# Two products a key chunk instead of three in the second batch's attention, with the sums of the exponentials taken by VectorE

## The chip, the core and the metric

The kernel runs on one core of one Trainium2 chip. The metric is the device time in microseconds (us) of one execution; the kernel before takes 920.13 us, the median of 3 runs (919.63 to 921.04).

## The reference, cut to what matters

Three layers follow each other: an attention whose queries are averaged in pairs, a mixture of four experts (w1, ReLU, w2, weighted by `domain_probs`), and a gated layer (`w_gate`, `w_val`, `w_out`). The change is in the first:

```
B, H, S, D = 2, 8, 1152, 64
q_pool = q.reshape(B, H, S // 2, 2, D).mean(axis=3)
scores = scale * np.matmul(q_pool, k.transpose(0, 1, 3, 2))
scores = scores - np.max(scores, axis=-1, keepdims=True)
attn = np.exp(scores)
attn = attn / (np.sum(attn, axis=-1, keepdims=True) + 1e-09)
return np.matmul(attn, v)
```

So every query needs a weighted sum of the values (the numerator) and the sum of its exponentials (the denominator).

## The kernel before

**Work and stages.** Products are made exact enough by splitting an fp32 operand into a high half (type F32R) and a low half, the rest. The attention is cut into 32 units `u`: 16 for each batch, each one head and 288 of its 576 pooled queries. A unit has its 1152 keys in nine chunks `c` of 128 partitions, so a score tile `s` holds 9 x 288 numbers a partition, in three groups `g` of three chunks. In order, a unit goes through `scores` (two products a chunk), `copy_scores` (ScalarE), `max_scores` (VectorE), `turn_max`, `reduce_max` and `spread_max` (the maximum over all keys, transposed and spread by TensorE), `subtract`, `expo`, and `av`, the product with the values. The experts of a batch (1536 products in all, `experts`, through the helper `gemm` at L864) need that batch's whole attention. The first batch's experts run beside the second batch's attention; then the second batch's experts run alone, and then the gated layer.

**The products with the values (L588).** In the first batch one plain fp32 product a chunk is made: the stationary tile holds 64 columns of values beside 64 columns of ones, so that the same product gives the numerator in 64 rows of the result and the denominator in the other 64. In the second batch, exponentials and values are split (`half_hi`, `half_lo` give `eh` and `el`; `prep_v` gives the halves of the values), and three F32R products a chunk are made: `vh`·`eh`, `vl`·`eh`, `vh`·`el`. `vh` has 64 columns of ones beside the high halves and `vl` 64 columns of zeros beside the low halves (`open_v`, L390, fills them by GpSimd). `take_part` (L608) then moves the numerator (ScalarE, tile `num`) and the denominator plus 1e-9 (VectorE, tile `den`) out of PSUM; after two units, `invert` makes the reciprocal of `den` (VectorE, two halves) and `scale` multiplies (GpSimd, into `xst`). `split_x` (L343) splits `xst` for the experts, for the second batch on ScalarE and VectorE.

**The order of the work.** Inside `tc.manual_schedule()` (L1097) the class `Plan` writes out one order for every engine. Each step is entered with a due time, an engine, a planned cost in us and its tiles (`at`, L60). `arrange` (L101) then simulates the engines: whenever one is free it takes, among the steps that are ready, the one due first. Steps that are ready are not held back for their due time (SP's loads are), so due times are priorities. The steps of unit `u` are due at `9 * u` plus one of the constants at L27 to L39; the `n`-th expert product of the first batch is due at `E0_START + n / E0_RATE` (L1103). A step's due time is never earlier than that of the steps whose tiles it reads or writes. Tiles with one buffer are handed on in the order of the due times (`takes`): PSUM bank `d` passes from `turn_max` to `spread_max` and to the transposes of the next keys and queries, bank `c` holds the running `av`, and there are three score tiles `s`. Steps marked `port` are kept from overlapping each other on VectorE and GpSimd in the simulation. The engines then run their lists in order. The second batch's experts and the gated layer come after the plan, in a fixed order.

Of the kernel before, what the change touches and what calls it, by code (L numbers as in the profile page):

```python
# [21 lines left out]
TOP = (1.875 - 2.0**-23) * 2.0**-96  # L22
# [1 line left out]

MT, TOP, MB, MCOPY = 10.23, 11.11, 11.18, 12.05  # L27
SUB = (11.07, 10.75, 13.58)
EXP = ((13.43, 16.94, 15.82), (12.68, 14.5, 17.57))
HALF_HI = (14.41, 16.21, 16.25)  # L30
HALF_LO = (13.1, 15.0, 17.1)
AV = (17.93, 15.5)
FINISH = (22.33, 24.2)
SHARE = (0.7, 2.54, 2.4, 3.2, 3.7)
COPY, MAX = 0.94, 0.25
PREP_Q, PREP_K = (4.3, 5.58, 0.4), (6.33, -0.27)
SPLIT = (-9.69, -6)
E0_START = 159.71
E0_RATE = 9.69  # L39
LAST = 18  # L40


class Plan:
# [8 lines left out]
    def __init__(self, room):  # L52
        self.room = room
        self.psum = ("sc", "av", "m")

        self.shared = ("v", "vh", "vl")
# [107 lines left out]
def tile_kernel(  # L164
# [13 lines left out]
    nc = tc.nc  # L178
    P = 128
    B, H, S, D = q.shape  # L180
# [4 lines left out]
    W = 288  # L185
# [3 lines left out]
    KC = S // P  # L189
    NPAIR = H // 2  # L190
# [29 lines left out]
    def single(tag, name):  # L220
        return psum.tile([P, 512], F32, tag=tag, name=name)
# [113 lines left out]
    at = plan.at  # L335
# [5 lines left out]
    vts, vlos = {}, {}  # L341

    def split_x(b, j, sl, hi=True, lo=True):  # L343
        if b not in xts:
# [13 lines left out]
    def where(u):  # L358

        jj, r = divmod(u, 2 * NH)  # L360
        half, i = divmod(r, 2)
        return jj // NPAIR, jj, half, i
# [27 lines left out]
    def open_v(which, i):  # L390

        tiles = vlos if which else vts
        tiles[f"h{i}"] = t = raw.tile(
            [P, KC, 2, D], F32R, tag=f"v{2 * which + i}", name=f"v{'hl'[which]}{i}"
        )
        nc.gpsimd.memset(t[:, :, 1 - i, :].bitcast(F32), 0.0 if which else 1.0)

    def prep_v(jj, i, lower):
        vr = vraws[jj, i]
        hi = vts[f"h{i}"][:, :, i, :]  # L400
        if not lower:
            nc.scalar.activation(out=hi, in_=vr, func=AF.Copy)
            return
        nc.gpsimd.tensor_tensor(
            out=vlos[f"h{i}"][:, :, i, :], in0=vr, in1=hi.bitcast(F32), op=ALU.subtract
        )


    spare = [acc.tile([QT, 2, NQT, 2 * D], F32, tag="acc", name="qraw1")]
# [178 lines left out]
    def av(u, chunks):  # L588
        b, jj, _, i = where(u)
        if u not in avs:  # L590
            avs[u] = single("c", "av")
        for c in chunks:
            if b:
                hi, lo = (h[:, c % 3, :] for h in parts[u, c // 3])
                vh, vl = vts[f"h{i}"], vlos[f"h{i}"]
                terms = [(vh, hi), (vl, hi), (vh, lo)]
            else:
                terms = [(vts[jj % 2 * 2 + i], stiles[u][:, c, :])]
            for n, (w, e) in enumerate(terms):
                nc.tensor.matmul(  # L600
                    avs[u][:, :W],
                    w[:, c].rearrange("p t d -> p (t d)"),
                    e,
                    start=(c == 0 and n == 0),
                    stop=(c == KC - 1 and n == len(terms) - 1),
                )

    def take_part(u, n):  # L608

        i = where(u)[3]  # L610
        name = ("num", "den")[n]
        if i == 0:
            pairs[u // 2, n] = small.tile([P, W], F32, tag=name, name=f"{name}{u}", bufs=1)
        me, other = slice(i * D, (i + 1) * D), slice((1 - i) * D, (2 - i) * D)
        t = pairs[u // 2, n][me]
        if n:
            nc.vector.tensor_scalar_add(t, avs[u][other, :W], EPS)
        else:
            nc.scalar.activation(out=t, in_=avs[u][me, :W], func=AF.Copy)

    def invert(u, n):
        den = pairs[u // 2, 1]
# [13 lines left out]
    def plan_attention():  # L636
# [61 lines left out]
        for u in range(B * UPB):  # L698
            t = KC * u
# [44 lines left out]
            for g in range(3):  # L744
                chunks = range(3 * g, 3 * g + 3)
                at(
                    t + SUB[g], "POOL" if g else "DVE", 2.05 if g else 1.05, subtract, u, g,
                    kind="port" if g else None,
                    reads=[("mc" if g else "m", u)], writes=[("s", u, c) for c in chunks],
                    uses=[("S", u)],  # L750
                )
                at(
                    t + EXP[b][g], "ACT", 0.925, expo, u, g,
                    writes=[("s", u, c) for c in chunks], uses=[("S", u)],
                )
# [14 lines left out]
                for cs in [chunks] if b == 0 else [[c] for c in chunks]:  # L770
                    at(
                        t + AV[b] + cs[0], "PE", 1.46 if b == 0 else 0.397, av, u, cs,
                        kind="r" if b else "f",
                        reads=[("eh", u, g), ("el", u, g), ("vh", i), ("vl", i)]
                        if b
                        else [("s", u, c) for c in cs] + [("v", jj % 2 * 2 + i)],
                        writes=[("av", u)],
                        takes=[("c", ("av", u))] if cs[0] == 0 else [],
                        uses=[("S", u)],
                    )  # L780
            end = t + FINISH[b]
            p = u // 2
            for n in range(2):
                tag = ("num", "den")[n]
                at(
                    end, ("ACT", "DVE")[n], (0.405, 0.455)[n], take_part, u, n,
                    reads=[("av", u)], writes=[(tag, p, i)], takes=[] if i else [(tag, (tag, p, 2))],
                    uses=[(tag, p, 2)],
                )
            if i == 1:  # L790
                for n in range(2):
# [45 lines left out]
        for jj in range(NPAIR, B * NPAIR):  # L837
            t = 4 * KC * jj
            for i in range(2):
                ready = t + 6.7 + KC * i  # L840
                at(
                    ready - 7, "SP", 0.5, load_vraw, jj, i,
                    writes=[("vr", jj, i)], takes=[("vraw", ("vr", jj, i))],
                )
                if jj == NPAIR:
                    for which, when in enumerate((20, 0.2)):
                        at(
                            ready - when, "POOL", 0.58, open_v, which, i,
                            takes=[(f"v{2 * which + i}", ("V", which, i))],
                            writes=[("v", 2 * which + i)],  # L850
                        )
                at(
                    ready, "ACT", 0.68, prep_v, jj, i, False,
                    reads=[("vr", jj, i), ("v", i)], writes=[("vh", i)],
                )
                at(
                    ready, "POOL", 1.45, prep_v, jj, i, True, kind="port",
                    reads=[("vr", jj, i), ("vh", i), ("v", 2 + i)], writes=[("vl", i)],
                )
# [321 lines left out]
```

## Time and profile before

| what | us |
|---|---|
| median of 3 runs | 920.13 |
| the profiled execution's own time | 921.15 |
| its span in the trace | 919.4 |
| TensorE busy in the span | 884.4 |
| VectorE busy | 576.6 |
| ScalarE busy | 462.0 |
| GpSimd busy | 388.4 |

The profile names the engines PE (TensorE; PEld is its weight load, which overlaps), DVE (VectorE), ACT (ScalarE), POOL (GpSimd) and SP (SyncE, which issues the loads). A group of instructions is printed as line, engine, operation, output and inputs, shapes, count, busy time and the mean duration of one in ns; behind the bar stands the engine's idle time just before them and what ended it. The duration that is printed for one matmul spans its passage through the array, and consecutive ones overlap; the time that a matmul takes from the engine is read from a run of them.

### The profile page before, as it was taken

The page shows a single profiled execution, that of the slowest core. Times are in us where ns is not written, and L with a number is a line of the kernel's source. Part 1 is how long each engine was busy: PE and PEld are TensorE (multiplying, and loading weights), DVE is VectorE, ACT ScalarE, POOL GpSimd, SP SyncE. Part 2 cuts the span into 40 slices and gives each one's busy share as a digit, 9 for nine tenths or more (in the row PEclk, how much of TensorE's full clock was granted, in tenths as well). Part 3 has the DMA queues.
Part 4 walks back from the last instruction along what each step waited for, and adds up shares of the span by engine and source line. Part 5 has one row for each costly group of instructions (what it writes and reads, how often), then busy time and mean ns, then how long its engine had stood idle before and what let it go on. Part 6 is the DMA issues. An engine that isn't in the chain of part 4 may idle for free.

```text
span 919.4 us, 14986 instructions
## 1 busy us (share of the span) xinstructions
PE 884.4 (96%) x5916; PEld 842.3 (92%) x5916; DVE 576.6 (63%) x883; ACT 462.0 (50%) x786; POOL 388.4 (42%) x266
## 2 busy tenths in 40 slices
PE   4899998999999999999999999999999999999998
PEld 3667777899999999999999999999999999999886
DVE  4678778776667577675664334333468988888800
ACT  4678778877776767666633222232323333333110
POOL 2465657867776796778631000203023333222000
PEclk9999999999999999999999999999999999999999
DMA  5012221323233223111243232323333323223210
GB/s 141 2 41 67 49 74 39 101 71 86 72 84 92 65 73 83 46 59 60 60 148 96 89 95 81 94 88 87 92 93 99 107 70 91 92 77 98 78 69 34
DMA packets 124149, 72.30 MB, mean 79 GB/s; under 512 B 32304, under 2 KB 119344, under 8 KB 124080
## 3 DMA queue, kind: packets, MB, share of 16 engines
q1 hardware_dynamic: 124080, 71.36, 26.7%
q8 instruction: 46, 0.75, 0.3%
q14 instruction: 23, 0.19, 0.1%
HBM read 68.96 MB, written 2.38 MB: 78 GB/s over the span
## 4 chain that ended last, share of the span: by engine, by line
PE 89%; DVE 5%; ACT 3%; issue 2%; DMA 1%; POOL 1%; SPq 0%; DVEq 0%; ACTq 0%; POOLq 0%
PE ps L864 43%; PE g L864 16%; PE av L600 12%; PE o L864 8%; PE sc L494 3%; PE sc L495 3%; DVE acc L522 1%; PE mt L528 1%; ACT s L511 1%; PE tr L438 1%; PE tr L464 1%; DVE kt L456 1%; PE m L550 1%; ACT s L573 1%; DVE s L567 1%
## 5 line engine op out<-in xcount | busy, mean ns | idle before, releaser
L306 ACT ACTIVATE whi<-wraw 128x512 fp32r<-128x512 f32 x128 | 80.4, 629 | 174.6 <-PE ps L864 157.1
L567 POOL TENSOR_TENSOR s<-s,m 128x864 f32<-128x864 f32 x64 | 132.2, 2085 | 76.3 <-ACT m L560 76.2
L864 PE MATMUL ps<-xhi,whi 128*128 128x288 f32 x512 | 153.0, 299 | 0.0
L864 PE MATMUL ps<-hhi,whi 128*128 128x288 f32 x512 | 152.2, 297 | 0.0
L864 PE MATMUL ps<-hhi,wlo 128*128 128x288 f32 x512 | 151.1, 295 | 0.0
L864 PE MATMUL ps<-xhi,wlo 128*128 128x288 f32 x512 | 151.0, 295 | 0.0
L864 PE MATMUL ps<-xlo,whi 128*128 128x288 f32 x512 | 150.9, 295 | 0.0
L864 PE MATMUL ps<-hlo,whi 128*128 128x288 f32 x512 | 150.9, 295 | 0.0
L313 DVE TENSOR_TENSOR wlo<-wraw,whi 128x512 fp32r<-128x512 f32 x96 | 81.9, 853 | 101.1 <-ACT whi L306 101.1
L931 POOL TENSOR_TENSOR yacc<-yacc,yt 128x576 f32<-128x576 f32 x24 | 41.3, 1722 | 187.8 <-DVE yt L925 187.8
L511 ACT ACTIVATE s<-sc 128x576 f32<-128x576 f32 (+1 forms) x160 | 93.5, 600 | 47.6 <-PE sc L495 45.9
L573 ACT ACTIVATE s<-s 128x864 f32<-128x864 f32 x96 | 87.7, 921 | 18.4 <-DVE s L567 13.8
L864 PE MATMUL g<-yhi,wlo 128*128 128x384 f32 x288 | 96.3, 334 | 0.5 <-DVE wlo L313 0.5
L864 PE MATMUL g<-yhi,whi 128*128 128x384 f32 x288 | 96.2, 334 | 0.5 <-ACT yhi L1022 0.5
L864 PE MATMUL g<-ylo,whi 128*128 128x384 f32 x288 | 96.2, 334 | 0.0
L864 PEld LDWEIGHTS ps<-xlo,whi 128*128 128x128 f32 x512 | 96.2, 188 | 0.0
L864 PEld LDWEIGHTS ps<-hlo,whi 128*128 128x128 f32 x512 | 96.1, 188 | 0.0
L864 PEld LDWEIGHTS ps<-hhi,whi 128*128 128x128 f32 x512 | 96.1, 188 | 0.0
L864 PEld LDWEIGHTS ps<-xhi,whi 128*128 128x128 f32 x512 | 96.1, 188 | 0.0
L864 PEld LDWEIGHTS ps<-xhi,wlo 128*128 128x128 f32 x512 | 96.1, 188 | 0.0
L864 PEld LDWEIGHTS ps<-hhi,wlo 128*128 128x128 f32 x512 | 96.1, 188 | 0.0
L494 PE MATMUL sc<-qhi,kt 128*128 128x288 f32 x288 | 88.2, 322 | 4.7 <-ACT s L511 1.9
(94 smaller groups left out, 1950.7 us busy)
## 6 DMA issues: line engine op xcount, KB each, us to landing
wraw<-in_moe_w_dram SPq DMA_DIRECT2D x128, 256.0 KB, 2.7
w<-in_moe_w_gate_dram SPq DMA_DIRECT2D x12, 512.0 KB, 3.9
w<-in_moe_w_val_dram SPq DMA_DIRECT2D x12, 512.0 KB, 3.6
w<-in_moe_w_out_dram SPq DMA_DIRECT2D x12, 512.0 KB, 3.5
qraw<-in_q_dram SPq DMA_DIRECT2D x32, 144.0 KB, 2.4
kraw<-in_k_dram SPq DMA_DIRECT2D x14, 288.0 KB, 3.9
v<-in_v_dram SPq DMA_DIRECT2D x8, 288.0 KB, 4.2
vraw<-in_v_dram SPq DMA_DIRECT2D x8, 288.0 KB, 3.0
```

What stands on the lines that cost most here:

```text
L306: nc.scalar.activation(out=hi, in_=t, func=AF.Copy)
L313: eng.tensor_tensor(out=lo, in0=t, in1=hi.bitcast(F32), op=ALU.subtract)
L438: nc.tensor.matmul(pt[:, m * P : (m + 1) * P], kr[:, c].rearrange("p h d -> p (h d)"), ident, is_transpose=True,)
L456: nc.vector.tensor_tensor(out=kt[other, sl], in0=pt[me, : 3 * P], in1=kt[me, sl].bitcast(F32), op=ALU.subtract)
L494: nc.tensor.matmul(ps, wt, qhi, start=True, stop=False)
L495: nc.tensor.matmul(ps, wt, qlo, start=False, stop=True)
L511: nc.scalar.activation(out=s[:, c : c + n, :], in_=ps[:, :n, :W], func=AF.Copy)
L567: eng.tensor_tensor(out=sg, in0=sg, in1=m.unsqueeze(1).to_broadcast([P, 3, W]), op=ALU.subtract)
L573: nc.scalar.activation(out=sg, in_=sg, func=AF.Exp)
L600: nc.tensor.matmul(avs[u][:, :W], w[:, c].rearrange("p t d -> p (t d)"), e, start=(c == 0 and n == 0), stop=(c == KC - 1 and n == len(term ...
L864: nc.tensor.matmul(ps, w, x, start=first and n == 0, stop=last and n == len(terms) - 1)
L931: nc.gpsimd.tensor_tensor(out=y, in0=y, in1=yts[o], op=ALU.add)
```

## The change

Second batch only: `vl` and the ones go. One tile per head of the pair holds the high halves of the values in 64 columns and the low halves in the other 64, and each chunk gets two products, with `eh` and with `el`. The two 64-row halves of the result are added when they leave PSUM: ScalarE copies one into `num`, VectorE adds the other. The denominator is now made from the score tile itself: `sum_keys` (VectorE) sums over the nine chunks into a 128 x 288 tile, `sum_half` splits this sum (ScalarE and VectorE), and `spread_sum` multiplies both halves by a 128 x 128 tile of ones (TensorE, two products, into bank `d`), so that every row holds the sum over all keys. Of the constants at L27 to L40 nearly all but `LAST` have new values, for both batches.

```diff
-SUB = (11.07, 10.75, 13.58)
-EXP = ((13.43, 16.94, 15.82), (12.68, 14.5, 17.57))
-AV = (17.93, 15.5)
-FINISH = (22.33, 24.2)
-SHARE = (0.7, 2.54, 2.4, 3.2, 3.7)
-E0_START = 159.71
-E0_RATE = 9.69
+SUB = (11.51, -9.28, 17.84)
+EXP = ((15.64, 16.94, 21.56), (15.03, 13.73, 23.95))
+AV = (17.65, 16.97)
+FINISH = (22.84, 24.44)
+SUMS = (15.3, 16.08, 23.47, 17.24)
+SHARE = (3.03, 2.61, 8.07, -3.95, 8.47)
+E0_START = 164.09
+E0_RATE = 10.72
...
     def prep_v(jj, i, lower):
+        if jj == NPAIR and not lower:
+            vts[f"h{i}"] = raw.tile([P, KC, 2, D], F32R, tag=f"v{i}", name=f"vh{i}")
...
         nc.gpsimd.tensor_tensor(
-            out=vlos[f"h{i}"][:, :, i, :], in0=vr, in1=hi.bitcast(F32), op=ALU.subtract
+            out=t[:, :, 1 - i, :], in0=vr, in1=hi.bitcast(F32), op=ALU.subtract
         )
+    def open_sums(i):
+        if i:
+            esum["all"] = raw.tile([P, W], F32, tag="v3", name="esum")
+            return
+        t = raw.tile([P, 2 * W + P], F32R, tag="v2", name="ehalves")
+        esum["hi"], esum["lo"], esum["ones"] = t[:, :W], t[:, W : 2 * W], t[:, 2 * W :]
+        nc.gpsimd.memset(esum["ones"].bitcast(F32), 1.0)
+    def sum_keys(u):
+        nc.vector.tensor_reduce(
+            out=esum["all"],
+            in_=stiles[u].rearrange("p c w -> p w c"),
+            axis=AX.X,
+            op=ALU.add,
+        )
+    def sum_half(lower):
+        hi = esum["hi"]
+        if not lower:
+            nc.scalar.activation(out=hi, in_=esum["all"], func=AF.Copy)
+            return
+        nc.vector.tensor_tensor(
+            out=esum["lo"], in0=esum["all"], in1=hi.bitcast(F32), op=ALU.subtract
+        )
+    def spread_sum(u):
+        mts["e", u] = ps = single("d", "es")
+        gemm(ps[:, :W], [(esum["ones"], esum[n]) for n in ("hi", "lo")])
...
-                vh, vl = vts[f"h{i}"], vlos[f"h{i}"]
-                terms = [(vh, hi), (vl, hi), (vh, lo)]
+                terms = [(vts[f"h{i}"], hi), (vts[f"h{i}"], lo)]
...
+        if n == 1:
+            src = mts["e", u][me, :W] if b else avs[u][other, :W]
+            nc.vector.tensor_scalar_add(t, src, EPS)
+        elif n == 0:
+            nc.scalar.activation(out=t, in_=avs[u][other if b else me, :W], func=AF.Copy)
         else:
-            nc.scalar.activation(out=t, in_=avs[u][me, :W], func=AF.Copy)
+            nc.vector.tensor_tensor(out=t, in0=avs[u][me, :W], in1=t, op=ALU.add)
...
-                        t + AV[b] + cs[0], "PE", 1.46 if b == 0 else 0.397, av, u, cs,
+                        t + AV[b] + cs[0], "PE", 1.46 if b == 0 else 0.265, av, u, cs,
...
+                at(
+                    t + SUMS[0], "DVE", 2.75, sum_keys, u,
+                    reads=[("s", u, c) for c in range(KC)] + [("sums", 1)], writes=[es],
+                    uses=[("S", u)],
+                )
+                at(
+                    t + SUMS[1], "ACT", 0.41, sum_half, False,
+                    reads=[es, ("sums", 0)], writes=[("eshi",)],
+                )
+                at(
+                    t + SUMS[2], "DVE", 0.45, sum_half, True, kind="port",
+                    reads=[es, ("eshi",)], writes=[("eslo",)],
+                )
+                at(
+                    t + SUMS[3], "PE", 0.265, spread_sum, u, kind="r",
+                    reads=[("eshi",), ("eslo",)], writes=[("dn", u)],
+                    takes=[("d", ("dn", u))],
+                )
...
+                    end + 0.1, "DVE", 0.455, take_part, u, 2,
...
-                ready = t + 6.7 + KC * i
+                ready = t + max(6.7, AV[1] - 9.9) + KC * i
```

The other constants go, in the order of L27 to L39: `MT, TOP, MB, MCOPY` to 0.94, 6.78, 12.36, 1.52; `HALF_HI` to 13.91, 16.58, 18.4; `HALF_LO` to 0.59, 14.46, 8.59; `COPY, MAX` to -10.71, -0.97; `PREP_Q`, `PREP_K` to (3.59, -20.08, -0.92), (7.29, -8.79); `SPLIT` to (-4.58, -0.84).

## Rows read from the trace of the kernel before

**Rows 1.** The page's header and first part: busy time and instructions by engine.

```profile
span 919.4 us, 14986 instructions
...
PE 884.4 (96%) x5916; PEld 842.3 (92%) x5916; DVE 576.6 (63%) x883; ACT 462.0 (50%) x786; POOL 388.4 (42%) x266
```

**Rows 2.** Windows by stage: length, busy us per engine (instructions), granted clock, DMA.

```profile
20.00:140.00 120.00, 106.44 (x596) 85.69 (x597) 90.26 (x145) 92.51 (x163) 68.79 (x49) 0.99 0.20 50
140.00:160.00 20.00, 17.88 (x102) 14.71 (x101) 16.79 (x27) 17.44 (x32) 13.96 (x11) 1.00 0.15 45
160.00:176.60 16.60, 15.93 (x91) 12.65 (x90) 12.98 (x22) 13.70 (x24) 11.76 (x11) 1.00 0.38 104
176.60:467.20 290.60, 290.39 (x2227) 289.90 (x2227) 195.94 (x256) 201.56 (x327) 209.59 (x128) 1.00 0.25 71
467.20:487.20 20.00, 20.00 (x153) 20.00 (x152) 11.79 (x16) 6.63 (x12) 9.00 (x7) 1.00 0.53 163
487.20:680.00 192.80, 192.80 (x1457) 192.80 (x1456) 75.50 (x111) 56.90 (x95) 18.88 (x11) 1.00 0.30 89
```

**Rows 3.** The chain in order of time: start us, us, engine, tile, instructions.

```profile
454.51 0.80 PE av L600 x6
...
467.24 210.69 PE ps L864 x1590
```

**Rows 4.** Groups by line, shapes apart: one of three groups of second-batch products.

```profile
L600 PE MATMUL av<-eh,vl 128*128 128x288 f32 x144 | 42.4, 295 | 0.0
```

**Rows 5.** Groups by line, shapes apart: VectorE and ScalarE operations nearest to the new ones.

```profile
L567 DVE TENSOR_TENSOR s<-s,m 128x864 f32<-128x864 f32 x32 | 33.5, 1048 | 7.3 <-ACT m L560 7.1
...
L522 DVE TENSOR_TENSOR acc<-sc,acc 128x576 f32<-128x576 f32 x64 | 47.9, 749 | 10.7 <-ACT s L511 9.8
...
L289 DVE SCALAR_TENSOR_TENSOR bits<-up,bits 128x512 int32<-128x512 int32 x72 | 53.2, 739 | 1.1
...
L538 DVE TENSOR_REDUCE top<-mt 96x3 f32<-96x384 f32 x32 | 17.6, 550 | 15.6 <-PE mt L528 15.5
...
L617 DVE TENSOR_SCALAR den<-av 64x288 f32<-64x288 f32 x32 | 14.6, 455 | 8.7 <-ACT num L619 8.0
...
L480 DVE SCALAR_TENSOR_TENSOR qlo<-tr,qhi 128x288 fp32r<-128x288 f32 x32 | 13.9, 434 | 10.1 <-ACT qhi L475 10.0
...
L475 ACT ACTIVATE qhi<-tr 128x288 fp32r<-128x288 f32 x32 | 12.9, 404 | 2.7 <-PE tr L464 2.5
...
L239 DVE TENSOR_TENSOR pn<-praw,total 128x9 f32<-128x9 f32 x4 | 0.5, 183 | 0.0
...
L234 DVE TENSOR_REDUCE total<-praw 128x9 f32<-128x36 f32 x1 | 0.2, 192 | 4.0 <-DMA praw<-in_moe_domain_probs_dram 4.0
```

**Rows 6.** One tile's instructions, el: shortest, median and longest ns by engine.

```profile
L585 POOL TENSOR_TENSOR el<-s,eh x32: 2047/2062/2510, 180.3 to 455.6; 128x864 fp32r<-128x864 f32 x32
L585 DVE TENSOR_TENSOR el<-s,eh x16: 1045/1492/2131, 177.2 to 450.2; 128x864 fp32r<-128x864 f32 x16
```

**Rows 7.** Timeline from the second batch's last product with the values on.

```profile
467.28 0.41 ACT L619 ACTIVATE num<-av 64x288 f32<-64x288 f32 x1 [2.68 <-PE av L600]
...
467.72 0.45 DVE L617 TENSOR_SCALAR den<-av 64x288 f32<-64x288 f32 x1 [2.40 <-ACT num L619]
468.20 0.76 DVE L925 TENSOR_TENSOR yt<-ps,pb 128x576 f32<-128x576 f32 x1
468.87 1.96 DVE L624 RECIPROCAL den<-den 128x144 f32<-128x144 f32 x2
...
471.32 0.83 POOL L632 TENSOR_TENSOR xst<-num,den 128x288 f32<-128x288 f32 x1
...
472.24 0.67 ACT L351 ACTIVATE xhi<-xst 128x576 fp32r<-128x576 f32 x1
...
473.30 0.75 DVE L354 TENSOR_TENSOR xlo<-xst,xhi 128x576 fp32r<-128x576 f32 x1
...
487.16 0.76 DVE L925 TENSOR_TENSOR yt<-ps,pb 128x576 f32<-128x576 f32 x1 [1.29 <-PE ps L864]
```

More of the change, by code (lines that the diff above doesn't have):

```diff
@@ L23 @@
 SIGN = -0x80000000
-MT, TOP, MB, MCOPY = 10.23, 11.11, 11.18, 12.05
-SUB = (11.07, 10.75, 13.58)
-EXP = ((13.43, 16.94, 15.82), (12.68, 14.5, 17.57))
-HALF_HI = (14.41, 16.21, 16.25)
-HALF_LO = (13.1, 15.0, 17.1)
-AV = (17.93, 15.5)
-FINISH = (22.33, 24.2)
-SHARE = (0.7, 2.54, 2.4, 3.2, 3.7)
-COPY, MAX = 0.94, 0.25
-PREP_Q, PREP_K = (4.3, 5.58, 0.4), (6.33, -0.27)
-SPLIT = (-9.69, -6)
-E0_START = 159.71
-E0_RATE = 9.69
+MT, TOP, MB, MCOPY = 0.94, 6.78, 12.36, 1.52
+SUB = (11.51, -9.28, 17.84)
+EXP = ((15.64, 16.94, 21.56), (15.03, 13.73, 23.95))
+HALF_HI = (13.91, 16.58, 18.4)
+HALF_LO = (0.59, 14.46, 8.59)
+AV = (17.65, 16.97)
+FINISH = (22.84, 24.44)
+SUMS = (15.3, 16.08, 23.47, 17.24)
+SHARE = (3.03, 2.61, 8.07, -3.95, 8.47)
+COPY, MAX = -10.71, -0.97
+PREP_Q, PREP_K = (3.59, -20.08, -0.92), (7.29, -8.79)
+SPLIT = (-4.58, -0.84)
+E0_START = 164.09
+E0_RATE = 10.72
 LAST = 18
@@ L54, in __init__ @@
         self.psum = ("sc", "av", "m")
-        self.shared = ("v", "vh", "vl")
+        self.shared = ("v", "vh", "vl", "sums")
         self.items = []
@@ L340, in tile_kernel @@
     kts, qts, stiles, accs, avs, pairs, ms, parts, tops, mts = ({} for _ in range(10))
-    vts, vlos = {}, {}
+    vts = {}
     def split_x(b, j, sl, hi=True, lo=True):
@@ L388, in load_vraw @@
         nc.sync.dma_start(out=vr, in_=values(jj, i))
[L390 to L396, printed above, removed]
     def prep_v(jj, i, lower):
+        if jj == NPAIR and not lower:
+            vts[f"h{i}"] = raw.tile([P, KC, 2, D], F32R, tag=f"v{i}", name=f"vh{i}")
         vr = vraws[jj, i]
-        hi = vts[f"h{i}"][:, :, i, :]
+        t = vts[f"h{i}"]
+        hi = t[:, :, i, :]
         if not lower:
@@ L404, in prep_v @@
         nc.gpsimd.tensor_tensor(
-            out=vlos[f"h{i}"][:, :, i, :], in0=vr, in1=hi.bitcast(F32), op=ALU.subtract
+            out=t[:, :, 1 - i, :], in0=vr, in1=hi.bitcast(F32), op=ALU.subtract
         )
+    esum = {}
+    def open_sums(i):
[23 more added lines that the diff above has]
+        gemm(ps[:, :W], [(esum["ones"], esum[n]) for n in ("hi", "lo")])
     spare = [acc.tile([QT, 2, NQT, 2 * D], F32, tag="acc", name="qraw1")]
@@ L608, in take_part @@
     def take_part(u, n):
-        i = where(u)[3]
-        name = ("num", "den")[n]
-        if i == 0:
+        b, _, _, i = where(u)
+        name = ("num", "den", "")[n]
+        if i == 0 and n < 2:
             pairs[u // 2, n] = small.tile([P, W], F32, tag=name, name=f"{name}{u}", bufs=1)
         me, other = slice(i * D, (i + 1) * D), slice((1 - i) * D, (2 - i) * D)
-        t = pairs[u // 2, n][me]
-        if n:
-            nc.vector.tensor_scalar_add(t, avs[u][other, :W], EPS)
+        t = pairs[u // 2, n % 2][me]
+        if n == 1:
[3 more added lines that the diff above has]
+            nc.scalar.activation(out=t, in_=avs[u][other if b else me, :W], func=AF.Copy)
         else:
-            nc.scalar.activation(out=t, in_=avs[u][me, :W], func=AF.Copy)
+            nc.vector.tensor_tensor(out=t, in0=avs[u][me, :W], in1=t, op=ALU.add)
     def invert(u, n):
@@ L782, in plan_attention @@
             p = u // 2
+            if b:
+                es = ("es",)
+                at(
[16 more added lines that the diff above has]
+                )
             for n in range(2):
@@ L785, in plan_attention @@
                 at(
-                    end, ("ACT", "DVE")[n], (0.405, 0.455)[n], take_part, u, n,
-                    reads=[("av", u)], writes=[(tag, p, i)], takes=[] if i else [(tag, (tag, p, 2))],
+                    t + SUMS[3] + 0.15 if b and n else end,
+                    ("ACT", "DVE")[n], (0.405, 0.455)[n], take_part, u, n,
+                    reads=[("dn" if b and n else "av", u)], writes=[(tag, p, i)], takes=[] if i else [(tag, (tag, p, 2))],
                     uses=[(tag, p, 2)],
+                )
+            if b:
+                at(
+                    end + 0.1, "DVE", 0.455, take_part, u, 2,
+                    reads=[("av", u)], writes=[("num", p, i)], uses=[("num", p, 2)],
                 )
@@ L845, in plan_attention @@
                 if jj == NPAIR:
[L846 to L851, printed above, removed]
+                    at(
+                        ready - 0.2, "POOL", 0.2, open_sums, i,
+                        takes=[(f"v{2 + i}", ("V", 1, i))],
+                        writes=[("sums", i), ("v", 2 + i)],
+                    )
                 at(
                     ready, "ACT", 0.68, prep_v, jj, i, False,
-                    reads=[("vr", jj, i), ("v", i)], writes=[("vh", i)],
+                    reads=[("vr", jj, i)],
+                    writes=[("vh", i)] + ([] if jj > NPAIR else [("v", i)]),
+                    **{"uses" if jj > NPAIR else "takes":
+                       [("V", 0, i) if jj > NPAIR else (f"v{i}", ("V", 0, i))]},
                 )
@@ L857, in plan_attention @@
                     ready, "POOL", 1.45, prep_v, jj, i, True, kind="port",
-                    reads=[("vr", jj, i), ("vh", i), ("v", 2 + i)], writes=[("vl", i)],
+                    reads=[("vr", jj, i), ("vh", i)], writes=[("vl", i)], uses=[("V", 0, i)],
                 )
```

## The prediction

> **What bounds the kernel now.** I read the page's first part first, then the span by stages, then the chain that ended last, then groups and timelines of the one stage that the change touches. TensorE is busy 884.4 of 919.4 us, VectorE 576.6 [rows 1]. That is an average, so the stages count. From 176.6 us on, where the first batch's experts begin, TensorE is busy 290.39 of 290.60 us until the attention's last product, then 20.00 of 20.00 and 192.80 of 192.80 us [rows 2]. Its weight loads fill these stretches as well, and the granted clock is 1.00. Before 176.6 us it has holes: 106.44 of 120 us, 17.88 of 20 and 15.93 of 16.6. The chain in order of time says the same: after 454.5 us it runs along TensorE, and one piece of it is 1590 products in 210.69 us without a break, 0.1325 us each [rows 3]. So in the second batch's attention the length of the stage is the sum of TensorE's work, and every product taken out there shortens the kernel, as long as the other engines deliver in time. In the same 290.60 us VectorE is busy 195.94 us (67%), ScalarE 201.56 (69%), GpSimd 209.59 (72%) [rows 2].
>
> **Removed.** Of three groups of 144 products (16 units of nine chunks) one goes, the one with the low halves of the values [rows 4]. The 295 ns of its row is passage, not cost; at 0.1325 us each, 144 products are 19.1 us. Three memsets of GpSimd fewer and smaller ones cost or bring nothing, since GpSimd is not the bound.
>
> **Added to TensorE.** `spread_sum`: 16 units with two products, 32 x 0.1325 = 4.2 us. Net, TensorE loses 112 products: 14.8 us.
>
> **Added to VectorE, per unit.** (1) `sum_keys` over 9 x 288 = 2592 numbers. No row of before has such a sum with a stride of 288 numbers, so I bound it. Two operations over 864 and 576 numbers take 1048 and 749 ns: 1.04 ns a number and 0.15 us fixed, which gives 2.84 us; the reduce over 384 numbers takes 550 ns, the same line [rows 5]. The dearest row per number of plain work, 739 ns for 512, gives 3.74 us. The row nearest in its kind is the reduce, so I take 2.84 us. The planner enters 2.75, and its other entries fit their rows (0.455 for `den`, 455 ns measured). (2) `sum_half`, low half, 288 numbers from two tiles: 0.45 us by the row of `qlo`, 434 ns. (3) the second addition in `take_part`: 0.455 us by the row of `den`. Together 3.75 us, 60 us in 16 units. ScalarE gets 16 x 0.404 = 6.5 us [rows 5].
>
> **Does the cover hold?** TensorE's mixed stretch was 176.6 to 487.2 us, where the last expert result is evicted [rows 7]: 310.6 us, and less 14.8 us it is 295.8 us. By due times the attention now ends nearer to the end of the experts: the last `av` is due at 279 + 16.97 + 8 = 304.0 and the last product at 164.09 + 1533 / 10.72 = 307.1, 33 products or 4.4 us later. Before, it was 302.5 against 317.9, 149 products or 19.8 us, and the trace shows 20.0 us from 467.2 to 487.2 [rows 2, 7], so due times are a good guide here. The attention therefore has 295.8 - 4.4 = 291 us, as many as before, and VectorE must do in them 195.9 us, most of the expert work that lay in the last 20 us (some 9 of 11.79), and 60 us: 265 us, 91%. ScalarE comes to about 73%. VectorE fits, but with little air. No row shows TensorE stalled by an engine so full. Cost of this: from nothing (every wait lands on steps with slack, and TensorE has two kinds of work to choose from) to 7 us (if VectorE can be driven no further than the 89% that TensorE itself reached from 20 to 140 us, 265 / 0.89 = 298 us). I take 0.5 us, near nothing, since three score tiles and four banks of running results lie between the two engines.
>
> **The new waits.** `sum_half` on VectorE waits for ScalarE's half; behind it in VectorE's list stand the experts' evictions and weight halves, for which TensorE waits. `spread_sum` on TensorE waits for that low half, with all products behind it. `copy_scores` of unit u + 3 waits for `sum_keys` of unit u, since both use the same score tile. Bank `d` gets one more holder per unit, so a late sum holds up the next maximum and the next transposes. `sum_half` also reads two SBUF tiles while GpSimd works: `el`, which does so, takes 1045 ns at best and 1492 in the median [rows 6], so up to 0.5 us more may come to each, inside the 91% and the 7 us above. The value loads are due 0.37 later, with 7 due units ahead of use: nothing.
>
> **The start of the experts** is due 4.4 units later, at some 1.09 us each (156.6 us for the first batch's 144): 4.8 us in which TensorE has attention alone. At the 4 to 11% idle that the stretches before show [rows 2] this costs 0.2 to 0.5 us. If second-batch units alone had to fill it, they have 38 products (5.0 us) against four GpSimd steps of 2.06 us [rows 6], and 40% of it or 1.9 us stood idle. I take 1.0.
>
> **The end of the attention.** From the last `av` the old chain ran `num` at 467.28, `den`, an expert's eviction, the reciprocals at 468.87 for 1.96 us, `xst` at 471.32, `xhi`, and `xlo` until 474.05 [rows 7]: 6.8 us, with 20 us of experts as cover. Now the denominator no longer comes from `av`, so `den` (0.45) and the reciprocals leave the chain, and the addition (0.455) enters it: 4.1 to 4.9 us, by whether an eviction stands in between. The cover is 4.4 us and nine products of the next experts that do not need this head pair (1.2 us). It holds by about 1 us; if the attention is late, the difference is paid in full. I take 0.7, with 0 and 5 as ends.
>
> **The first batch** does the same work in an order from new constants. Its stretch holds 16.4 us of TensorE's holes [rows 2], so it can go either way by a few us; I take nothing, with 3 either way.
>
> **Sum.** 921.15 of the profiled execution, less 14.8, plus 0.5 + 1.0 + 0.7: 908.5 us. That execution lies 1.0 above the median, so the forecast is 907.5 us.
>
> **The rivals.**
> *VectorE late.* At 91% its waits reach TensorE, in gaps of part of a microsecond behind evictions or at the end of the attention. For it: the long `sum_keys` stands in front of short steps that TensorE needs. Against it: TensorE waited for nothing at 67%. Price up to 7 us: 908 to 915.
> *The first batch in its new order.* 3 us or more lost or won there: 903 or 912, and further out 918. Its holes speak for it.
> *VectorE becomes the bound: slower.* Mechanism: the strided read of `sum_keys`. VectorE has 291 us and 220 us of other work by the sum above, so 71 us remain, 4.5 us for each sum; beyond that VectorE sets the stage, and from about 5.4 us on (all 14.8 us given back) the kernel is slower than before. At twice my price, 5.7 us, VectorE has 311 us, at 95% use 327 us against 291: some 36 us more than forecast, about 940 us; with the experts done early, still over 925. The rows hardly decide: all long VectorE operations read neighbours; only `pn` steps, by four numbers, and takes 183 ns for nine, where the reduce over 36 neighbours takes 192 [rows 5], so fixed cost hides it. Against it stands the planner's 2.75. [...]
> *Nothing is released.* The products are gone but TensorE's stretch stays as long, because something else paces it. Against it: its weight loads and products fill 100% of it, and no row shows another pace. About 920.
>
> **How the numbers follow.** Forecast 0.60, VectorE late 0.23, first batch 0.08 (of it 0.01 slower and 0.01 the same), VectorE as bound 0.06, nothing released 0.03. Within 0.2% (1.8 us, about what a measurement of this kernel can tell) is 0.04, slower 0.07, faster 0.89; I move 0.02 from faster to slower for mishaps in a full rewrite of the order, which the rows can't price. The range takes in the forecast, the late VectorE and most of the first batch: 903 to 916 us, with about 0.15 outside.
>
> **What would show it.** Right: `sum_keys` near 2.8 us, TensorE still full from the experts' start on, some 2115 products in a stretch shorter by 14 us, VectorE near 90% there. Wrong: `sum_keys` beyond 4 us; TensorE's idle time behind evictions, `wlo`, `eslo` or `xlo`; the experts starting after 185 us; or holes near the end of the attention.

## The result, and the profile after

The changed kernel takes 933.62 us (median of 4 runs, 932.23 to 935.2) against 920.59 us before: 1.0143 times as long, with an interval of 1.0125 to 1.0162. It is slower by 13 us where 12.6 us less were forecast. These are the span, the busy times and the granted clock in 40 slices of the changed kernel's page, answering to [rows 1]:

```profile
span 931.7 us, 14800 instructions
...
PE 880.1 (94%) x5804; PEld 832.2 (89%) x5804; DVE 666.9 (72%) x931; ACT 465.5 (50%) x802; POOL 393.9 (42%) x263
...
PEclk9999999989999999999999999999999999999999
```

TensorE is busy for 880.1 us, 4.3 less than before where 14.8 less were reckoned, VectorE for 90 us more where 60 were reckoned, and in one slice the granted clock is below nine tenths. The windows of the changed kernel, cut as in [rows 2] at the experts' first product (174.9 us), at the first sum (182.4), before the last reciprocals (493) and behind the last expert eviction (499.6):

```profile
20.00:140.00 120.00, 106.77 (x600) 86.04 (x599) 90.42 (x146) 92.45 (x164) 68.89 (x48) 0.99 0.20 50
140.00:160.00 20.00, 17.80 (x102) 14.35 (x101) 17.43 (x28) 17.66 (x34) 13.77 (x11) 1.00 0.11 32
160.00:174.90 14.90, 14.10 (x83) 11.84 (x82) 10.98 (x19) 11.90 (x21) 10.99 (x10) 1.00 0.48 131
174.90:182.40 7.50, 7.50 (x60) 7.50 (x59) 6.65 (x11) 6.86 (x13) 5.78 (x5) 1.00 0.28 82
182.40:493.00 310.60, 293.23 (x2166) 286.50 (x2165) 284.31 (x301) 203.11 (x338) 217.20 (x129) 0.98 0.24 68
493.00:499.60 6.60, 6.60 (x51) 6.53 (x50) 6.47 (x9) 4.08 (x7) 2.79 (x3) 1.00 0.46 140
```

and two windows of 20 us inside this stretch:

```profile
180.00:200.00 20.00, 17.48 (x110) 16.79 (x109) 16.39 (x21) 12.84 (x23) 12.74 (x10) 0.83 0.19 58
260.00:280.00 20.00, 18.01 (x127) 17.81 (x126) 13.91 (x20) 10.99 (x19) 10.83 (x6) 0.91 0.25 68
```

The first batch costs what it did: 106.77 of 120 us and 17.80 of 20 stand against 106.44 and 17.88 in [rows 2]. The loss is all between the experts' first product and their end: 324.7 us, where the same stretch took 310.6 us before and TensorE had hardly a hole in it. From the first sum to the last reciprocals TensorE is idle for 17.4 us of 310.6 (0.2 us in the 290.6 us of [rows 2]), and VectorE is busy for 284.31 us, 92%. These are the groups of the new steps, by line and shape:

```profile
L417 DVE TENSOR_REDUCE esum<-s 128x288 f32<-128x2592 f32 x16 | 79.1, 4941 | 0.1
...
L429 DVE TENSOR_TENSOR ehalves<-esum,ehalves 128x288 fp32r<-128x288 f32 x16 | 15.4, 965 | 0.0
...
L647 DVE TENSOR_SCALAR den<-es 64x288 f32<-64x288 f32 x16 | 7.3, 454 | 6.4 <-PE es L924 6.2
...
L651 DVE TENSOR_TENSOR num<-av,num 64x288 f32<-64x288 f32 x16 | 7.2, 451 | 0.3
L427 ACT ACTIVATE ehalves<-esum 128x288 fp32r<-128x288 f32 x16 | 7.1, 444 | 41.8 <-DVE esum L417 41.8
```

The sum takes 4.94 us and not 2.84. The low half of the sum takes 0.97 us and not 0.45. The two small additions take what their row of before said (454 and 451 ns against 455), and ScalarE's half a tenth more (444 ns against 404 in [rows 5]). The chain that ended last, in the stretch from 182 to 196 us, in order of time, and behind it one line of TensorE's timeline, shows how a sum reaches TensorE:

```profile
182.40 4.80 DVE esum L417
...
187.23 0.56 DVE top L568
...
187.84 0.74 PE m L580 x3
188.58 0.53 PE sc L524
189.11 0.24 PE sc L525
189.35 0.24 PE sc L524
```

```profile
187.84 0.74 PE L580 MATMUL m<-ident,top 96*128 96x96 f32 x3 [2.45 <-DVE top L568]
```

The maximum of a later unit (`top`) stands behind the sum in VectorE's list, the product that spreads it (`m`) waits for `top`, and all of TensorE's list stands behind that product: 2.45 us idle. This is the longest hole. What TensorE waits for from 174.9 to 499.6 us (us in total, times, longest) shows the others:

```profile
PE mt L558 <- DVE acc L549: 7.6, 5, 2.1
PE sc L524 <- DVE acc L552: 3.5, 4, 1.7
PE m L580 <- DVE top L568: 3.5, 3, 2.5
```

Of 16.9 us, 14.6 go by these three waits, for VectorE's running maximum (`acc`, of `max_scores`) and for `top`; the eight holes of 0.8 us and more among them all end 0.5 to 2.3 us behind a sum on VectorE. The score products behind the first hole also show what comes after it: start to start they take 0.24 us instead of 0.1325, and the granted clock is 0.50 from 187.84 to 194.2 us (0.83 over this window) and 1.00 from 194.2 to 200. Over the whole stage, the shares of this chain read as follows (the first line of the same view, from 174 to 500 us):

```profile
by line: PE ps L924 25.9%; DVE esum L417 13.3%; issue 10.3%; PE av L629 4.2%; DVE den L656 3.7%; PE sc L524 3.4%; DVE wlo L314 3.3%; PE sc L525 2.9%; DVE acc L552 2.6%; DVE kt L486 2.2%; ACT s L603 2.1%; POOL s L597 2.1%; DVE el L615 1.9%; 
```

Before, the chain was TensorE's alone but for 0.8%; the same line of that kernel, from 176.6 to 467.2 us:

```profile
by line: PE ps L864 63.3%; PE av L600 19.4%; PE sc L494 5.7%; PE sc L495 5.6%; PE mt L528 1.8%; PE m L550 1.3%; PE tr L464 1.1%; PE tr L438 1.0%; DVE kt L456 0.4%; ACT kt L454 0.3%; issue 0.1%
```

At the end, VectorE's timeline answers to [rows 7]:

```profile
484.05 4.92 DVE L417 TENSOR_REDUCE esum<-s 128x288 f32<-128x2592 f32 x1
...
492.54 0.46 DVE L647 TENSOR_SCALAR den<-es 64x288 f32<-64x288 f32 x1
493.03 1.97 DVE L656 RECIPROCAL den<-den 128x144 f32<-128x144 f32 x2
495.03 0.46 DVE L651 TENSOR_TENSOR num<-av,num 64x288 f32<-64x288 f32 x1
...
499.54 0.76 DVE L985 TENSOR_TENSOR yt<-ps,pb 128x576 f32<-128x576 f32 x1
```

The last sum runs until 489.0 us, and `den` and the reciprocals still come after it. The forecast had taken them out of the end of the chain.

### The profile page after: what moved, and what is told of

It reads as the page before. It is cut to its first block, busy times and chain, and to the rows that moved or that the text cites. A ratio compares the mean times of both kernels' runs of the same rounds, so it can differ in the third digit from the quotient of the medians.

```text
span 931.7 us, 14800 instructions
## 1 busy us (share of the span) xinstructions
PE 880.1 (94%) x5804; PEld 832.2 (89%) x5804; DVE 666.9 (72%) x931; ACT 465.5 (50%) x802; POOL 393.9 (42%) x263
## 4 chain that ended last, share of the span: by engine, by line
PE 68%; DVE 19%; issue 5%; ACT 5%; POOL 2%; DMA 1%; SPq 0%; DVEq 0%; ACTq 0%; POOLq 0%
PE ps L924 29%; PE g L924 16%; PE o L924 8%; PE av L629 7%; DVE esum L417 5%; PE sc L524 3%; DVE acc L552 2%; PE sc L525 2%; DVE wlo L314 1%; ACT s L541 1%; DVE kt L486 1%; ACT s L603 1%; DVE den L656 1%; PE mt L558 1%; POOL s L597 1%
## 5 line engine op out<-in xcount | busy, mean ns | idle before, releaser
L597 POOL TENSOR_TENSOR s<-s,m 128x864 f32<-128x864 f32 x64 | 136.7, 2157 | 63.6 <-ACT m L590 63.6
L314 DVE TENSOR_TENSOR wlo<-wraw,whi 128x512 fp32r<-128x512 f32 x96 | 78.2, 814 | 86.5 <-ACT whi L307 86.5
```

Source lines behind the costliest of these rows:

```text
L314: eng.tensor_tensor(out=lo, in0=t, in1=hi.bitcast(F32), op=ALU.subtract)
L597: eng.tensor_tensor(out=sg, in0=sg, in1=m.unsqueeze(1).to_broadcast([P, 3, W]), op=ALU.subtract)
```

## The experiments

Theory A: the distance of 288 numbers makes the sum dear, and a VectorE without room holds up TensorE. Theory B: nine numbers a result are dear as such. Theory C: the new order and its waits cost the time, whatever a sum takes. All ratios are against the kernel before on the same chip (921.3 to 921.7 us; 920.6 for the change itself).

### The price of the sum inside the kernel: neighbours, five chunks, seven chunks

```diff
-            in_=stiles[u].rearrange("p c w -> p w c"),
+            in_=stiles[u].rearrange("p c w -> p (c w)").rearrange("p (w c) -> p w c", c=KC),
```

> The changed kernel, but each of the 288 results sums nine neighbouring numbers of the score tile instead of nine that lie 288 apart: the same count of numbers and of results, the same order of work; the denominators are not those of the reference. Theory A (the distance of the numbers makes the sum dear, and VectorE's fullness makes the stage long): one sum takes 2.7 to 2.9 us instead of 4.94, TensorE's idle time from the experts' start to their end falls from some 17 us to under 5, and the kernel takes 905 to 912 us. Theory B (sums of nine are dear because each result starts anew): still 4.9 us a sum and 930 to 935 us. Theory C (the new order and its added waits cost the time, whatever a sum takes): about 2.8 us a sum, but 920 us or more.

```diff
-            in_=stiles[u].rearrange("p c w -> p w c"),
+            in_=stiles[u][:, :5].rearrange("p c w -> p w c"),
```

> The changed kernel, but the sum takes only the first five of the nine chunks, still 288 numbers apart; the denominators leave out four chunks. The planner's order is the same. Theory A: at 1.85 to 1.9 ns a number 1440 numbers take 2.75 to 2.85 us, which is what the planner reckoned with, and the kernel takes 905 to 912 us, as with neighbours. Theory B: some 16 ns a result at nine numbers; with five numbers a result between 2.6 us (the cost goes by the numbers) and 4 us (it goes by the results). Theory C: 920 us or more.

The third takes `[:, :7]` in the same place.

> The changed kernel with the sum over seven of the nine chunks, 288 apart; the denominators leave out two chunks. The price of a sum lies between the two known ones: at 1.9 ns a number 2016 numbers take 3.8 to 3.9 us. By the forecast's threshold (VectorE is the bound only from 4.5 us on, and the kernel slower than before from 5.4 on) the time stays near that of the cheap sums, 910 to 914 us. If VectorE's price is paid gradually (every us of a sum costs part of a us in each of the 16 units, from 2.84 us at 910 to 4.94 us at 933), it is 919 to 923 us. If VectorE is the bound at 4.94 us and each us costs 16 us, 915 to 918 us.

| a sum reads | one sum, us | kernel, us | ratio and interval |
|---|---|---|---|
| nine neighbours a result | 2.84 | 910.30 | 0.9877 (0.9862 to 0.9892) |
| five numbers, 288 apart | 2.84 | 909.89 | 0.9873 (0.9857 to 0.9889) |
| seven numbers, 288 apart | 3.91 | 919.39 | 0.9975 (0.9966 to 0.9985) |
| nine numbers, 288 apart (the change) | 4.94 | 933.62 | 1.0143 (1.0125 to 1.0162) |

The sum's lines and the window from 175 to 500 us with neighbours:

```profile
L417 DVE TENSOR_REDUCE esum<-s x16: 2791/2840/2854, 184.0 to 462.1; 128x288 f32<-128x2592 f32 x16
```

```profile
175.00:500.00 325.00, 322.56 (x2449) 319.19 (x2448) 283.73 (x340) 224.12 (x373) 225.03 (x135) 1.00 0.28 81
```

The same number of numbers and results, read side by side, takes 2.84 us, TensorE is idle for 2.4 of 325 us, and the kernel is 11 us faster than before. Five numbers 288 apart take the same time and give the same kernel. So B falls, and C in its plain form: the order, the waits and the added steps are worth most of the forecast's gain (11 us of 12.6) as long as a sum takes what the planner was told. Seven numbers show that in this order the price isn't paid from a threshold on: the first 1.07 us above 2.84 cost 9 us, the next 1.03 us 14 us. Between the last two lines of the table the kernel before is met at about 4.05 us (3.91 + 1.03 x 2.0 / 14.2).

### The sum by itself

> The kernel before, with sums and additions of a tile of 2592 numbers a partition put behind its last output, on a VectorE that is otherwise idle; each form three times, and two of them again while GpSimd works. [...] Theory B: 288 apart, neighbours, 2, 4 and 8 apart all near 4.9 us, nine long results 2.8. Should GpSimd's work be what stretches the sum, it takes 2.8 us beside an idle GpSimd and 4.9 beside a busy one. The four additions of neighbouring runs (1152, 576, 288, 288 numbers) take 1.3 + 0.7 + 0.4 + 0.4 = 2.8 us together.

```diff
+            nc.vector.tensor_reduce(out=out, in_=view, axis=AX.X, op=ALU.add)
...
+            v = big.rearrange("p (a c s) -> p a s c", c=9, s=n)
...
+            red(big.rearrange("p (c w) -> p w c", c=9))
...
+            red(big.rearrange("p (w c) -> p w c", c=9))
...
+            red(big.rearrange("p (c w) -> p c w", c=9), res[:, 0:9])
...
```

VectorE's timeline of this kernel behind its last output, in this order of forms (288 apart, neighbours, nine long results, 2, 4 and 8 apart, the four additions), and at the end 288 apart once more while GpSimd works:

```profile
918.34 4.50 DVE L1107 TENSOR_REDUCE pres<-pbig 128x288 f32<-128x2592 f32 x1
...
922.88 2.85 DVE L1107 TENSOR_REDUCE pres<-pbig 128x288 f32<-128x2592 f32 x1
...
925.76 2.85 DVE L1107 TENSOR_REDUCE pres<-pbig 128x9 f32<-128x2592 f32 x1
...
928.65 2.85 DVE L1107 TENSOR_REDUCE pres<-pbig 128x288 f32<-128x2592 f32 x1
...
931.54 4.74 DVE L1107 TENSOR_REDUCE pres<-pbig 128x288 f32<-128x2592 f32 x1
...
936.32 4.74 DVE L1107 TENSOR_REDUCE pres<-pbig 128x288 f32<-128x2592 f32 x1
...
941.09 1.36 DVE L1136 TENSOR_TENSOR pbig<-pbig 128x1152 f32<-128x1152 f32 x1
942.49 0.76 DVE L1137 TENSOR_TENSOR pbig<-pbig 128x576 f32<-128x576 f32 x1
943.28 0.46 DVE L1138 TENSOR_TENSOR pbig<-pbig 128x288 f32<-128x288 f32 x1
943.77 0.46 DVE L1139 TENSOR_TENSOR pbig<-pbig 128x288 f32<-128x288 f32 x1
...
998.71 4.57 DVE L1107 TENSOR_REDUCE pres<-pbig 128x288 f32<-128x2592 f32 x1
```

Neighbours, nine long results and numbers 2 apart (8 bytes) all take 2.85 us. At 4 and 8 apart (16 and 32 bytes) it is 4.74, at 288 apart 4.50. GpSimd's work beside it changes little (4.57). So of what was varied here the distance alone sets the price, and the price steps up between 8 and 16 bytes (2.85 against 4.74 us). Inside the changed kernel the same sum takes 4.94 us, 0.4 us more than on the quiet chip, while a sum of neighbours takes the same in both (2.84 and 2.85 us). Why this is so was not tried.

### The order: told the length, ordered for it, cut into thirds

```diff
-                    t + SUMS[0], "DVE", 2.75, sum_keys, u,
+                    t + SUMS[0], "DVE", 4.95, sum_keys, u,
```

> The changed kernel with one number changed: the planner is told 4.95 us for a sum instead of 2.75, so that its order fits the measured length. Theory A in its strict form (VectorE has no room left): the kernel stays over 920 us, between 922 and 934, with VectorE still over 90% busy in the stage. Rival (VectorE has room; the loss came from an order made for short sums, in which TensorE's list waits behind sums that end late): 908 to 918 us, with TensorE's idle time in the stage under 6 us.

928.52 us, 1.0078 times the kernel before (1.0052 to 1.0105): 5 us less than the change, still slower than before. The strict form of A seemed to hold. The next kernel keeps that edit and changes the constants as well:

```diff
-SUB = (11.51, -9.28, 17.84)
-EXP = ((15.64, 16.94, 21.56), (15.03, 13.73, 23.95))
-HALF_HI = (13.91, 16.58, 18.4)
-HALF_LO = (0.59, 14.46, 8.59)
-AV = (17.65, 16.97)
-E0_START = 164.09
-E0_RATE = 10.72
+SUB = (2.15, -9.28, 19.39)
+EXP = ((17.59, 16.94, 21.56), (15.03, 17.57, 23.96))
+HALF_HI = (13.91, 17.68, 19.91)
+HALF_LO = (0.59, 21.95, 9.05)
+AV = (17.38, 18.53)
+E0_START = 163.22
+E0_RATE = 10.58
...
```

> The changed kernel with the sum told at its measured length of 4.95 us, and with other planner constants, searched so that the planner's own simulation ends the first batch's experts as early as it can with that length. The work is the same instruction for instruction; only the order differs. If VectorE has no room for sums of 4.95 us (its total sets the length of the stage), the order can't help: 924 to 932 us, as when the length alone was told. If VectorE has room and it is the order, made for sums of 2.75 us, in which TensorE's list waits behind VectorE's, the kernel comes to 912 to 920 us, below the kernel before.

917.85 us, 0.9958 times the kernel before (0.9941 to 0.9975). Its sums and its window from 175 to 500 us:

```profile
L417 DVE TENSOR_REDUCE esum<-s x16: 4917/4999/5105, 182.8 to 468.3; 128x288 f32<-128x2592 f32 x16
```

```profile
175.00:500.00 325.00, 318.66 (x2400) 313.20 (x2399) 299.77 (x334) 223.34 (x367) 224.68 (x135) 1.00 0.27 78
```

What TensorE waits for there, over the same 325 us, for the running maximum:

```profile
PE sc L524 <- DVE acc L552: 1.3, 2, 0.8
PE mt L558 <- DVE acc L549: 0.3, 1, 0.3
```

The sums are as dear as in the change (5.0 us), VectorE is as full (299.77 us, 92%; 94% up to the end of this kernel's own experts at 484.8 us), and yet TensorE is idle for 6.3 us only: its waits for `acc` and `top` are down from 14.6 us to 1.6. So most of the loss, 933.6 to 917.9, was not a lack of room on VectorE: it was an order made for sums of 2.75 us. Telling the planner the length brought 5 of these 16 us, new due times the rest. What is left to the cheap sums, 917.9 to 910, is 8 us; 4 of them are TensorE's idle time (6.3 against 2.4 us), and the rest is open. The kernel is also a little faster than the one before, by 3.7 us.

> The same strided sum in three steps of 96 results each, planned at 1.7 us a step, with constants searched in the same way. VectorE does the same work, without a step longer than 2 us. If long uninterrupted steps in front of the short ones that TensorE waits for are what is left of the loss, this is faster than the reordered kernel by 3 us or more: 907 to 914 us. If only VectorE's total counts, it is within 2 us of it.

```diff
+        sl = slice(n * W // 3, (n + 1) * W // 3)
         nc.vector.tensor_reduce(
-            out=esum["all"],
-            in_=stiles[u].rearrange("p c w -> p w c"),
+            out=esum["all"][:, sl],
+            in_=stiles[u][:, :, sl].rearrange("p c w -> p w c"),
...
```

920.43 us (917.7 to 921.59 in 10 runs), 0.9986 (0.9974 to 0.9997): not faster than the reordered kernel but 2.6 us slower. A third takes 1.76 us, 84 us in all against 80. So cutting the sum didn't bring the 3 us that were expected if long steps were what is left. The run doesn't rule them out: its due times differ as well, and its sums take 4 us more in all.

### Other sums, and room elsewhere on VectorE

```diff
+        nc.vector.tensor_tensor(out=t, in0=s[:, 0:4], in1=s[:, 4:8], op=ALU.add)
+        nc.vector.tensor_tensor(out=t[:, 0:2], in0=t[:, 0:2], in1=t[:, 2:4], op=ALU.add)
+        nc.vector.tensor_tensor(out=t[:, 0], in0=t[:, 0], in1=t[:, 1], op=ALU.add)
+        nc.vector.tensor_tensor(out=t[:, 0], in0=t[:, 0], in1=s[:, 8], op=ALU.add)
```

> The changed kernel with the sum made of four additions of neighbouring runs (1152, 576, 288 and 288 numbers), planned as one step of 3.0 us that is kept from overlapping GpSimd's steps. Theory A: the additions take 3.04 us with GpSimd idle, 2 us less than the strided sum, and the kernel takes 908 to 916 us, less than both kernels. Rival: additions read two tiles, wait for GpSimd as el and wlo do, and lose what they win: over 4 us together and 918 us or more.

970.81 us, 1.0537 times the kernel before (1.0516 to 1.0559): the worst of all. The additions in that kernel, shortest, median and longest in ns:

```profile
L419 DVE TENSOR_TENSOR esum<-s x16: 1287/1347/2824, 184.1 to 520.8; 128x1152 f32<-128x1152 f32 x16
L420 DVE TENSOR_TENSOR esum<-esum x16: 757/1488/3651, 186.0 to 522.2; 128x576 f32<-128x576 f32 x16
L421 DVE TENSOR_TENSOR esum<-esum x16: 457/1428/2202, 189.7 to 524.0; 128x288 f32<-128x288 f32 x16
L422 DVE TENSOR_TENSOR esum<-esum,s x16: 457/459/2185, 190.2 to 524.5; 128x288 f32<-128x288 f32 x16
```

On the quiet chip these four took 1.36, 0.76, 0.46 and 0.46 us. Here the shortest are no longer than that, but the second and third take 1.4 to 1.5 us in the median and up to 3.7. They read two tiles of SBUF while GpSimd works (it is busy for 223.84 of the 345 us from 175 to 520 us), as `el` does in [rows 6]; the rival of this expectation is what happened. Which of the stretched additions lay beside a step of GpSimd was not shown for this kernel. The probe shows the stretch without the kernel: GpSimd starts there at 994.65 us, and an addition of 288 numbers takes 1.18 us instead of 0.46 beside it.

```profile
994.22 0.30 DVE L1144 COPY pgin<-pres 128x288 f32<-128x288 f32 x1
...
995.22 1.18 DVE L1138 TENSOR_TENSOR pbig<-pbig 128x288 f32<-128x288 f32 x1
...
997.64 1.03 DVE L1147 COPY pbig<-pgin 128x288 f32<-128x288 f32 x1
```

The strided sum, which reads one tile, doesn't spread like that (4.80 to 5.02 us in the changed kernel). One tile alone doesn't protect a step, though: a copy of 288 numbers takes 0.30 us before GpSimd starts and 1.03 beside it. The clock is a part of this kernel's loss too: its mean is 0.981 of 968.5 us against 0.993 of 931.7 in the change, by estimate 12 of the 37 us between them.

> As e4, with the four additions planned as steps of their own (1.35, 0.75, 0.45, 0.45 us), so that short steps that TensorE waits for can go in between. If the length of one uninterrupted step is what holds up TensorE, it is faster than e4 by 2 us or more; if only VectorE's total counts, within 2 us of e4, 908 to 916 us.

```diff
-                    t + SUMS[0], "DVE", 2.75, sum_keys, u,
...
+                for n, cost in enumerate((1.35, 0.75, 0.45, 0.45)):
+                    at(
+                        t + SUMS[0], "DVE", cost, sum_keys, u, n, kind="port",
...
```

943.28 us, 1.0238 (1.0223 to 1.0254): 27 us faster than in one step, as expected if a long step holds up TensorE, and still slower than the change.

> As e6, with den in the second batch copied by ScalarE instead of VectorE (the 1e-9 left out there: the sum is at least one, so fp32 does not see it). VectorE has 16 x 0.455 = 7.3 us less to do, ScalarE 16 x 0.405 = 6.5 us more. If VectorE's fullness still costs time in e6, this gains 1 to 5 us over it; if TensorE is the bound again, nothing, 905 to 910 us.

```diff
+            if b:
+                nc.scalar.activation(out=t, in_=mts["e", u][me, :W], func=AF.Copy)
...
```

946.31 us, 1.0262 (1.0242 to 1.0282). Taking `den` off VectorE brought nothing.

> The strided sum as in the change, told to the planner at 4.95 us, and VectorE relieved elsewhere: den of the second batch is copied by ScalarE, and in every second unit GpSimd makes the low half of the first group, too. VectorE loses 16 x 0.455 + 8 x 1.48 = 19 us, as much as if a sum cost 3.75 us. Theory A (it is VectorE's total that sets the length, wherever in it the time is saved): 910 to 918 us, below the kernel before. Rival (the long uninterrupted sum itself holds up TensorE, whatever room VectorE has): 922 us or more, like the kernel that was only told the length.

```diff
-        eng = nc.gpsimd if g else nc.vector
+        eng = nc.gpsimd if g or u % 2 else nc.vector
```

with the edit of the kernel before it to `den`, and the sum told at 4.95.

929.65 us, 1.0101 (1.0084 to 1.0117), against 928.52 with the length told alone. The edits take 19 us of steps off VectorE, but it is busy for only 8 us less from 160 to 520 us (315.09 us for 323.00), where GpSimd is busy for 17 us more (250.06 us for 232.97). What took the rest back was not shown. The kernel took as long, but so small a relief says little about room; the reordered kernel says more.

> The strided sum as in the change, told at 4.95 us, but what follows it is done on few numbers: TensorE multiplies the sum with one column of ones, so that a unit's 288 sums stand as 96 x 3, VectorE inverts those, TensorE spreads them over the partitions as it does with the maximum, and ScalarE copies them to den. VectorE loses the low half (0.97), the addition (0.455) and the reciprocals (1.04) and gets some 0.2: 2.3 us less a unit, 36 us in all, as much as if a sum cost 2.7 us. TensorE gets nine small products for two of 0.13 us, some 0.3 to 0.5 us more a unit, 5 to 8 us. Theory A: 908 to 917 us, and VectorE under 90% busy in the stage. Rival as for e9: 922 us or more.

```diff
+            nc.tensor.matmul(
+                ps[:QT, t : t + 1],
+                esum["all"][:, t * QT : (t + 1) * QT],
+                esum["ones"][:, 0:1],
...
+        nc.vector.reciprocal(esum["r"], mts["t", u][:QT, :NQT])
...
+                esum["r"][:, t : t + 1].to_broadcast([QT, P]),
+                ident[:QT, :QT],
+                is_transpose=True,
...
```

932.57 us, 1.0127 (1.0112 to 1.0142). Here VectorE did get room: 263.56 us of the 325 from 175 to 500 us, 81%. But TensorE got more to do, as the weight loads of the new products and the window show:

```profile
L426 PEld LDWEIGHTS et<-eones,esum 128*96 128x96 f32 x96 | 10.3, 168 | 1.1 <-DVE s L608 1.1
```

```profile
L442 PEld LDWEIGHTS es<-ident,rsum 96*128 96x128 f32 x48 | 5.8, 140 | 0.0
```

```profile
175.00:500.00 325.00, 315.96 (x2388) 310.13 (x2387) 263.56 (x291) 215.94 (x356) 218.84 (x134) 0.98 0.25 72
```

The products with one column of ones have weight loads of 168 ns each, six records a unit, and three transposes follow with loads of 140 ns. Together these loads are busy for 16.1 us, where the two products that they replace took 32 x 0.1325 = 4.2: by this estimate 12 us more for TensorE, not 5 to 8. It is busy for 315.96 us of 325, at a mean granted clock of 0.98. Whether the order suits these steps badly as well, the run doesn't separate. All five kernels of this part keep due times made for other steps; whether new ones would mend them was not tried.

## Why the prediction was wrong

**The step that failed** is the price of `sum_keys`: 2.84 us taken, 3.74 as the upper end, 4.94 measured. It was bounded by operations that all read neighbours, and the planner's 2.75 was read as support because other entries fit their rows. The rival that names the strided read, with 0.06, had the cause of the price right (at 5.7 us a sum), and the probe confirms it without the kernel around it; what it made of the price, VectorE as the bound, is not what the runs show, since the reordered kernel pays the same price and is faster than the kernel before. The chance of a dear sum should have been much larger: no row spoke against it.

**The threshold failed with it.** The forecast let VectorE be the bound from 4.5 us a sum and the kernel slower than before from 5.4. Measured in the change's order, the kernel is slower from about 4.05 us, and 3.91 us already cost 9 us. At 4.94 us the sum of work asks for 220 + 79 = 299 us of VectorE against 291, about 8 us more than forecast; the kernel took 26 more. A sum of VectorE's work leaves out that TensorE's list is fixed: every sum that ends later than planned delays the short steps behind it, and TensorE waits although both engines have time in hand. The reordered kernel shows this: same price, 92% of VectorE's time, 16 us less. The forecast had named the wait, in its rival of a late VectorE ("the long `sum_keys` stands in front of short steps that TensorE needs"), and had put 7 us on it at most; in its sum the whole cover stands with 0.5 us. In the changed kernel TensorE is idle for 17.4 us of the 325 us from 175 us on, and with sums of neighbours for 2.4.

**The clock** is a part of the loss that had no term: the granted clock was 0.83 and 0.91 in two windows of 20 us with holes in TensorE's work. By estimate a mean of 0.83 over 20 us is 3.4 us of full-speed work not done, 0.91 is 1.8 us. TensorE's longer idle time (17.4 against 2.4 us, as above) and these 5.2 us are together 20 of the 23 us between the changed kernel and the one that sums neighbours.

**What held.** TensorE's gain is real: with sums of 2.84 us the kernel takes 910.3 us, where 907.5 was forecast from that price. The first batch's new order costs nothing. The small additions cost what their rows said, and the low half of the sum paid the 0.5 us for GpSimd that was put down as possible (0.97 us in the mean: 0.44 to 0.45 in the six that GpSimd's steps overlap by under 0.3 us, 0.69 to 1.67 in the ten others). The start of the experts was wrong in sign: their first product starts at 174.9 us, 1.4 us earlier than before (176.35), not 4.8 later, so the due time is not what it hangs on. The end of the attention was wrong as well: `den` and the reciprocals stayed in it behind the last sum. It cost little, since TensorE is busy from 493 to 499.6 us without a break and idle for 0.4 us of the 20 us behind.

## What to carry to other kernels

Before a reduction goes to VectorE, look at the distance of the numbers that it reads one after the other, and measure it alone if no row of the trace has that distance; here 16, 32 and 1152 bytes made it 1.6 to 1.7 times as dear as 4 or 8 (4.50 to 4.74 us against 2.85). In a kernel whose order is written out from planned durations, a wrong duration costs time of its own (16 us here, at equal work): enter what was measured and order anew before judging the change. An engine at 92% of a stage need not be its bound; an order made for other lengths can be (933.6 us against 917.9, at 92% in both).

## What was not expected of the hardware

The step in VectorE's price lies between 8 and 16 bytes of distance (2.85 against 4.74 us for 2592 numbers), and 288 numbers apart is a little cheaper (4.50) than 4 or 8 apart. Additions of two SBUF tiles spread from 0.76 to 3.65 us for one and the same shape (576 numbers), in a kernel whose GpSimd was busy for 223.84 of 345 us. A copy of 288 numbers, which reads one tile, went from 0.30 to 1.03 us beside GpSimd's steps in the probe, while the strided sum hardly changed (4.50 to 4.57). And TensorE's granted clock, 1.00 over the whole stage before (176.6 to 467.2 us), was 0.50 for 6.4 us behind a hole of 2.45 us here (products followed each other at 0.24 us), and 1.00 behind one of 2.14 us that ended at 366.7 us (1.00 from 360 to 380 us).
